# Full 128x128 weights for the routing's counts and broadcasts on TensorE, and two shifted fill lengths

## The chip, the cores and the metric

The kernel runs on one core of a Trainium2 chip. The metric is the device time of one execution in microseconds (us); lower is better. The kernel before takes 982.31 us (median of three runs, 982.09 to 982.40). The core has five engines that run beside each other and meet at semaphores: PE (TensorE, matrix products; its weight loads are listed apart as PEld), DVE (VectorE), ACT (ScalarE), POOL (GpSimd) and SP, which only issues transfers.

## The reference

Three stages follow each other: a linear attention, a gated FFN, and a mixture of experts with a greedy assignment. The change touches the routing of the third, cut here to what matters:

```python
def _moe2_ref(x, w_gate, w1, w2):            # x 2304x512, E = 8 experts
    cap = N // E                              # 288 tokens for each expert
    logits = x @ w_gate
    order = np.argsort(-logits.flatten())
    for idx in order:                         # best (token, expert) pair first
        tok, e = int(idx) // E, int(idx) % E
        if assigned[tok] >= 0 or counts[e] >= cap:
            continue
        assigned[tok] = e
        counts[e] += 1
    for e in range(E):
        mask = assigned == e
        out[mask] = np.maximum(x[mask] @ w1[e], 0.0) @ w2[e]
```

## The kernel before

The tokens lie in 18 chunks of 128 (NC = 18), a token to a partition. The greedy loop is replaced by seven phases (function `route`). Each phase finds, for every expert, the threshold of the logit from which its tokens fit into what is left of its capacity. The threshold's bits are found digit by digit, in six steps: two digits of 6 bits, then four of 5 bits. A step does this:

- DVE makes the candidate thresholds (`cand`) and compares every token's logit with all C of them (`ge`, 18 chunks of C columns; C is 62, 63 and then four times 31).
- PE counts: 18 matmuls (line 173), one for each chunk, with C columns of `ge` as weights and the chunk's 8 columns of `O` (which expert the token wants) as moving operand. They add up in `cnt`, C x 8.
- DVE compares the counts with the room left (`ok`, line 175).
- PE adds up the `ok` flags and spreads the sum to all 128 partitions in one matmul (line 179, `num`), with weights of C rows and 128 columns, all equal to the digit's unit (`pw`), or ones.
- DVE takes the maximum (`dig`): that is the digit, and the next step's candidates start from it.

After the six steps a phase ends with full 128x128 weights (`ones`, `li`): lines 201, 204 and 206, 19 matmuls that count tokens and settle ties.

While DVE works on a step, PE has something else to do. The last matmul of the FFN (line 903, 648 matmuls `py` with 128x512 moving operands) is a generator, `filler`. `route` yields a length in ns at each point where PE would wait, and `fill` puts so many matmuls of line 903 there, one for each 233 ns, carrying the rest over to the next yield. FILL holds the lengths: [0] ahead of a phase's first count, [1] ahead of the second count (63 columns), [2] ahead of the four counts of 31 columns, [3] between a count and its `num`, [4] ahead of line 201. PE, DVE and ACT run this part in the order in which it is written. Where the routing ends, what is left of the 648 matmuls runs, and then the experts start. POOL and SP are ordered by a scheduler.

`room` is a buffer of the pool that holds `xh` (the FFN's input); the routing keeps the 5-bit `ge` and its last one-hot matrices there. `us` and `li` are triangles, loaded with one DMA (`tri`) into a staging buffer `ws` and cast by POOL.

Of the kernel before, what the change touches and what calls it, by code (L numbers as in the profile page):

```python
# [9 lines left out]
F32 = mybir.dt.float32  # L10
F32R = mybir.dt.float32r
BF = mybir.dt.bfloat16
I32 = mybir.dt.int32
AF = mybir.ActivationFunctionType
OP = mybir.AluOpType
# [5 lines left out]
NT, DM, FF, E, FE = B * S, 512, 1536, 8, 1024  # L21
CAP = NT // E
NC = NT // 128
SL = 96
NJ = CAP // SL
NSL = NT // SL
BLK = 512
# [3 lines left out]
KD = DM // 128  # L31
# [4 lines left out]
W_SCALE = 2.0 ** -112  # L36
DIGITS = (6, 6, 5, 5, 5, 5)
SHIFTS = (26, 20, 15, 10, 5, 0)
FILL = (4900, 2450, 1800, 466, 1400, 3900, 5600)
FILL_MM = 233  # L40

DW = 3
# [58 lines left out]
def route(nc, keep, sb, ps, cst, L, R, ids, slot, aside, room):  # L101
# [7 lines left out]
    ones, us, li, cf, ci = cst["ones"], cst["us"], cst["li"], cst["cf"], cst["ci"]  # L109
    A3 = [128, NC, E]  # L110
    parts, off = [], 0
    for n in (31, NSL, SL, 2 * NSL):
        parts.append(room[:, off:off + NC * n].rearrange("p (c n) -> p c n", c=NC))
        off += NC * n
    ge5, oa, ob, rt = parts
    rt = rt.rearrange("p c (a n) -> p c a n", a=2)
    asg = keep.tile(A3, BF, name="asg")
    rem = keep.tile([128, E], F32, name="rem")
# [21 lines left out]
    def settle():  # L140
        pass

    s, O = best(True)
    for phase in range(E - 1):
        fb = None
        off = 0
        for step, (dg, sh) in enumerate(zip(DIGITS, SHIFTS)):
            C = (1 << dg) - (1 if step else 2)
            row = ci[:, off:off + C]
            off += C  # L150
            if step:
                cand = sb.tile([128, C], I32, name=f"cand{dg}")
                if step == 1:
                    nc.vector.tensor_tensor(cand, row, fb.to_broadcast([128, C]), op=OP.bitwise_xor)
                else:
                    nc.vector.tensor_scalar(cand, row, dig[:, :1], fb[:, :1], op0=OP.bitwise_xor,
                                            op1=OP.bitwise_xor)
                    nf = sb.tile([128, 1], I32, name="fb")
                row = cand
            ge = ge5 if dg == 5 else sb.tile([128, NC, C], BF, name=f"ge{dg}", bufs=1)  # L160
            cnt = ps.tile([64, 512], F32, name="cnt", bufs=1)
            nc.vector.tensor_tensor(ge, s.unsqueeze(2).to_broadcast([128, NC, C]),
                                    row.bitcast(F32).unsqueeze(1).to_broadcast([128, NC, C]), op=OP.is_ge)
            if step > 1:
                nc.vector.tensor_tensor(nf, fb, dig, op=OP.bitwise_xor)
                fb = nf
            if step:
                aside()
            else:
                settle()  # L170
            yield FILL[0] if step == 0 else FILL[1] if dg == 6 else FILL[2]
            for c in range(NC):
                nc.tensor.matmul(cnt[:C, :E], ge[:, c, :], O[:, c, :], start=(c == 0), stop=(c == NC - 1))  # L173
            ok = sb.tile([64, E], BF, name="ok")
            nc.vector.tensor_tensor(ok[:C], cnt[:C, :E], rem[:C], op=OP.is_ge)
            yield FILL[3]
            num = ps.tile([128, 512], F32, name="num", bufs=1)
            dig = sb.tile([128, 1], I32, name="dig")
            nc.tensor.matmul(num[:, :E], (cst["pow"][sh] if step else ones)[:C], ok[:C], start=True, stop=True)
            if step == 0:  # L180
                mx = sb.tile([128, 1], F32, name="mx")
                nc.vector.tensor_reduce(out=mx, in_=num[:, :E], axis=AX.X, op=OP.max)
                nc.vector.tensor_scalar(dig, mx, 1.0 - float(1 << (dg - 1)), float(1 << sh), op0=OP.add,
                                        op1=OP.mult)
                sg = sb.tile([128, 1], I32, name="sg")
                nc.vector.tensor_scalar(sg, dig, 31, 0x7FFFFFFF, op0=OP.arith_shift_right, op1=OP.bitwise_and)
                fb = sb.tile([128, 1], I32, name="fb")
                nc.vector.tensor_tensor(fb, dig, sg, op=OP.bitwise_xor)
            else:
                nc.vector.tensor_reduce(out=dig, in_=num[:, :E], axis=AX.X, op=OP.max)  # L190
        ti = sb.tile([128, 1], I32, name="ti")
        nc.vector.tensor_tensor(ti, fb, dig, op=OP.bitwise_xor)
        th = ti.bitcast(F32)
        A = sb.tile(A3, BF, name="A")
        Q = sb.tile(A3, BF, name="Q")
        nc.vector.scalar_tensor_tensor(A, bc(s), th, O, op0=OP.is_ge, op1=OP.mult)
        nc.vector.scalar_tensor_tensor(Q, bc(s), th, O, op0=OP.is_equal, op1=OP.mult)
        yield FILL[4]
        tot = ps.tile([128, 512], F32, name="cnt", bufs=1)
        totv = tot[:, :NC * E].rearrange("p (c e) -> p c e", e=E)  # L200
        nc.tensor.matmul(totv, ones, A, start=True, stop=True)
        suf = ps.tile([128, 512], F32, name="num", bufs=1)
        sufv = suf[:, :NC * E].rearrange("p (c e) -> p c e", e=E)
        nc.tensor.matmul(sufv, li, Q, start=True, stop=False)
        for c in range(1, NC):
            nc.tensor.matmul(sufv[:, :c, :], ones, Q[:, c:c + 1, :].to_broadcast([128, c, E]), start=False,
                             stop=(c == NC - 1))
        n = sb.tile([128, E], F32, name="n")
        ex = sb.tile([128, E], F32, name="ex")
        cl = sb.tile([128, E], F32, name="cl")  # L210
        ce = sb.tile([128, E], F32, name="ce")
        rj = sb.tile(A3, BF, name="rj")
        tk = sb.tile([128, NC], F32, name="tk")
        nc.vector.tensor_reduce(out=n, in_=totv.rearrange("p c e -> p e c"), axis=AX.X, op=OP.add)
        nc.vector.tensor_sub(ex, n, rem)
        nc.vector.tensor_scalar(cl, ex, 0.0, 100.0, op0=OP.is_ge, op1=OP.mult)
        nc.vector.tensor_scalar(ce, ex, 0.0, -BIG, op0=OP.is_ge, op1=OP.mult)
        nc.vector.tensor_tensor(R, R, be(cl), op=OP.max)
        nc.vector.tensor_tensor(L, L, be(ce), op=OP.add)
        nc.vector.tensor_tensor(rj, sufv, be(ex), op=OP.is_le)  # L220
        nc.vector.tensor_mul(rj, rj, Q)
        nc.vector.tensor_sub(A, A, rj)
        s, O = best(phase < E - 2)
        nc.vector.tensor_reduce(out=tk, in_=A, axis=AX.X, op=OP.max)
        nc.vector.scalar_tensor_tensor(gone, tk, -BIG, gone, op0=OP.mult, op1=OP.add)
        if phase < E - 2:
            nc.vector.tensor_add(s, s, gone)

        def settle(A=A, n=n, cl=cl):
            nc.vector.tensor_tensor(n, n, rem, op=OP.min)  # L230
            nc.vector.tensor_sub(rem, rem, n)
            nc.vector.scalar_tensor_tensor(rem, cl, 1e7, rem, op0=OP.mult, op1=OP.add)
            nc.vector.tensor_add(asg, asg, A)
# [3 lines left out]
    nc.vector.tensor_add(asg, asg, A)  # L237
    yield FILL[5]
    pre = ps.tile([128, 512], F32, name="num", bufs=1)
    prev = pre[:, :NC * E].rearrange("p (c e) -> p c e", e=E)  # L240
    nc.tensor.matmul(prev, us, asg, start=True, stop=False)
    for c in range(NC - 1):
        nc.tensor.matmul(prev[:, c + 1:, :], ones, asg[:, c:c + 1, :].to_broadcast([128, NC - 1 - c, E]),
                         start=False, stop=(c == NC - 2))
# [9 lines left out]
    for j in range(2, NJ):  # L254
# [7 lines left out]
                            op=OP.mult)  # L262
# [5 lines left out]
    for c in range(NC):  # L268
        nc.tensor.matmul(pi[:SL, :2 * NSL], ob[:, c, :], rt[:, c].rearrange("p a b -> p (a b)"), start=(c == 0),
                         stop=(c == NC - 1))  # L270
# [16 lines left out]
def kernel(ctx, tc, qT, kT, v1, om, wgv, rms, wo, wg2, w1, w2, cfd, trd, cid, out, dbg=None):  # L287
    nc = tc.nc
# [3 lines left out]
    stage = ctx.enter_context(tc.tile_pool(name="stage", bufs=3))  # L292
# [400 lines left out]
    ws = stage.tile([128, 2 * M], F32, name="ws")  # L693
# [93 lines left out]
    rp = fc.enter_context(tc.tile_pool(name="rp", bufs=2))  # L787
    psB = fc.enter_context(tc.tile_pool(name="psB", bufs=2, space=PSUM))
    ci = rp.tile([128, cid.shape[1]], I32, name="ci", bufs=1)
    ones, us, li = (rp.tile([128, 128], BF, name=n, bufs=1) for n in ("ones", "us", "li"))  # L790
    pw = {sh: rp.tile([128, 128], BF, name=f"pw{sh}", bufs=1) for sh in SHIFTS[1:]}
    nc.sync.dma_start(ci, cid)
    nc.gpsimd.memset(ones, 1.0)
    tri = stage.tile([128, 256], F32, name="ws")
    nc.sync.dma_start(tri, trd[:, :256])
    nc.gpsimd.tensor_copy(us, tri[:, :128])
    nc.gpsimd.tensor_copy(li, tri[:, 128:])
    for sh in pw:
        nc.gpsimd.memset(pw[sh], float(1 << sh))
    wos, hts = [], {}  # L800

    def wo_split(c):
# [17 lines left out]
    lates, step = [], 0  # L820
# [15 lines left out]
    while True:  # L836
# [5 lines left out]
        j, f, v = ffn_step_el()  # L842
# [94 lines left out]
        nc.sync.dma_start(dbg["L"].rearrange("(c p) e -> p c e", p=128), L)  # L937
    xg = {}
    room = xp.tile([128, KD * BLK], F32, name="xh").bitcast(BF)
    hot = xp.tile([128, TAIL, CAP], F32R, name="xl")  # L940

    def gather(e, j):
# [36 lines left out]
    sb = ctx.enter_context(tc.tile_pool(name="sb", bufs=2))  # L979
    ps = ctx.enter_context(tc.tile_pool(name="psC", bufs=2, space=PSUM))  # L980
# [141 lines left out]
```

## Time and profile before

| | |
|---|---|
| median of 3 runs | 982.31 us (982.09 to 982.40) |
| the profiled execution's own time | 982.99 us |
| its span, first to last instruction | 981.2 us |
| PE busy | 960.6 us, 98% of the span |
| DVE / ACT / POOL busy | 54% / 39% / 23% |
| routing (start of the first count to start of the last matmul of line 206) | 548.0 to 724.0 us |

The span is what the rows count in, from the first instruction. Between it and the execution's own time lie 1.8 us. A busy PE is not a PE at its peak: a matmul's length in the profile overlaps the next one's, so distances between starts tell more than lengths.

### The profile page before, as it was taken

The numbers are of one execution on the slowest core, as the hardware profiler recorded it, in microseconds if no ns is written. First come the engines' busy times: TensorE is split into PE (matmuls) and PEld (weight loads), VectorE is DVE, ScalarE is ACT, GpSimd is POOL, SyncE is SP. The second block draws the span as 40 slices with busy tenths as digits, with TensorE's granted clock in tenths as the row PEclk, the third lists the DMA queues.
The fourth block names the chain that finished last, engine by engine and source line by source line (L and its number), as shares of the span: only waits on it lengthen the run. The fifth ranks groups of instructions, "written<-read, shape, count | busy, mean of one in ns | idle before, by whom it ended". The sixth has DMA issues, their size and how long they took to land.

```text
span 981.2 us, 16610 instructions
## 1 busy us (share of the span) xinstructions
PE 960.6 (98%) x6419; PEld 812.5 (83%) x6419; DVE 526.5 (54%) x1199; ACT 384.4 (39%) x897; POOL 228.4 (23%) x278
## 2 busy tenths in 40 slices
PE   9998999999999999999999999999999999999996
PEld 7777789888788687777779777777778999999996
DVE  4899866556423463232244556566563555666652
ACT  6976646545433444122233110000003444444441
POOL 2375512112322225224333000000004211112111
PEclk9999999989999999999999999999999999999999
DMA  8457634543131217225665566666543566666550
GB/s 295 154 167 233 198 119 137 183 127 97 47 110 61 87 51 262 107 96 182 209 200 173 148 187 171 201 177 174 171 128 94 164 188 194 187 199 193 173 171 29
DMA packets 117151, 153.15 MB, mean 156 GB/s; under 512 B 8272, under 2 KB 78544, under 8 KB 117072
## 3 DMA queue, kind: packets, MB, share of 16 engines
q1 hardware_dynamic: 111264, 137.80, 45.3%
q0 software_dynamic: 3072, 9.44, 3.1%
q10 hardware_dynamic: 2736, 4.85, 1.3%
q8 instruction: 50, 0.82, 0.3%
q14 instruction: 29, 0.24, 0.1%
HBM read 108.03 MB, written 44.04 MB: 155 GB/s over the span
## 4 chain that ended last, share of the span: by engine, by line
PE 71%; issue 18%; DVE 5%; POOL 4%; ACT 1%; DMA 0%; POOLq 0%; SPq 0%; ACTq 0%; DVEq 0%
PE py L903 16%; PE gv L598 10%; PE gv L600 10%; PE gv L599 10%; PE pm L464 3%; PE pm L419 3%; PE cnt L173 2%; POOL out_dram L1031 2%; PE pm L460 2%; PE pp L373 1%; PE pp L378 1%; PE pp L375 1%; PE pp L374 1%; POOL xh L947 1%; DVE dw L531 1%
## 5 line engine op out<-in xcount | busy, mean ns | idle before, releaser
L598 PE MATMUL gv<-xh,wc 128*128 128x512 f32 (+1 forms) x480 | 185.9, 387 | 3.2 <-DVE th L610 2.4
L599 PE MATMUL gv<-xl,wc 128*128 128x512 f32 (+1 forms) x480 | 184.5, 384 | 0.9 <-DVE xl L506 0.9
L600 PE MATMUL gv<-xh,wc 128*128 128x512 f32 (+1 forms) x480 | 184.6, 385 | 0.0
L903 PE MATMUL py<-wc,ht 128*128 128x512 f32 x648 | 174.6, 407 | 0.0
L903 PEld LDWEIGHTS py<-wc,ht 128*128 128x128 f32 x648 | 114.2, 188 | 20.9
L598 PEld LDWEIGHTS gv<-xh,wc 128*128 128x128 f32 x480 | 91.4, 190 | 21.6 <-DVE th L610 2.6
L385 ACT ACTIVATE ft<-pp,mx 128x128 f32<-128x128 f32 (+1 forms) x320 | 92.5, 373 | 37.2 <-DVE mx L382 36.5
L599 PEld LDWEIGHTS gv<-xl,wc 128*128 128x128 f32 x480 | 91.2, 190 | 16.0 <-DVE xl L506 1.2
L600 PEld LDWEIGHTS gv<-xh,wc 128*128 128x128 f32 x480 | 91.2, 190 | 15.7
L610 DVE SCALAR_TENSOR_TENSOR th<-th,gv 128x512 f32<-128x512 f32 (+1 forms) x60 | 37.9, 632 | 97.1 <-ACT th L609 97.1
L625 POOL TENSOR_TENSOR hp<-th,hp 128x512 fp32r<-128x512 f32 (+1 forms) x48 | 57.4, 1196 | 136.3 <-ACT hp L624 121.8
L874 DVE TENSOR_TENSOR wc<-ws,wc 128x512 fp32r<-128x512 f32 x128 | 84.8, 683 | 0.0
L1009 PE MATMUL ph<-exh,wc 128*128 128x288 f32 x256 | 77.5, 303 | 0.8 <-issue 0.8
L1019 PE MATMUL py<-ehh,wc 128*128 128x288 f32 x256 | 77.7, 304 | 0.0
L1011 PE MATMUL ph<-exh,wc 128*128 128x288 f32 x256 | 76.1, 297 | 0.0
L1020 PE MATMUL py<-ehl,wc 128*128 128x288 f32 x256 | 75.9, 297 | 0.0
L1021 PE MATMUL py<-ehh,wc 128*128 128x288 f32 x256 | 75.9, 296 | 0.0
L1010 PE MATMUL ph<-exl,wc 128*128 128x288 f32 x256 | 75.8, 296 | 0.0
L914 ACT COPY ys<-py 128x512 f32<-128x512 f32 x18 | 10.6, 587 | 165.2 <-PE py L903 164.7
L382 DVE TENSOR_REDUCE mx<-pp 128x4 f32<-128x512 f32 (+2 forms) x88 | 56.0, 637 | 29.9 <-PE pp L375 22.5
L884 ACT CAST wc<-ws 128x1024 fp32r<-128x1024 f32 x64 | 66.9, 1046 | 2.4 <-ACT ys L914 2.4
L622 DVE SCALAR_TENSOR_TENSOR th<-gv,th 128x512 f32<-128x512 f32 (+1 forms) x48 | 30.0, 624 | 53.2 <-PE gv L600 52.9
(199 smaller groups left out, 1802.5 us busy)
## 6 DMA issues: line engine op xcount, KB each, us to landing
ws<-in_w_dram SPq DMA_DIRECT2D x64, 512.0 KB, 3.6
ht<-h_dr SPq DMA_DIRECT2D x54, 512.0 KB, 4.1
h_dr<-hp SPq DMA_DIRECT2D x36, 512.0 KB, 2.8
ws<-in_wgv_dram SPq DMA_DIRECT2D x24, 512.0 KB, 4.5
h_dr<-hp SPq DMA_DIRECT2D x24, 256.0 KB, 2.9
ws<-in_wo_dram SPq DMA_DIRECT2D x12, 512.0 KB, 3.8
h_dr<-ht SPq DMA_DIRECT2D x12, 512.0 KB, 3.0
y_dr<-ys ACTq DMA_DIRECT2D x18, 256.0 KB, 4.3
```

What stands on the lines that cost most here:

```text
L385: nc.scalar.activation(ft[:n, g], pp[:n, g], AF.Exp, bias=mx[:n, g:g + 1])
L598: nc.tensor.matmul(pg[:, :n], w[:, 0, v, k], xh[:, k, :n], start=(k == 0), stop=False)
L599: nc.tensor.matmul(pg[:, :n], w[:, 0, v, k], xl[:, k, :n], start=False, stop=False)
L600: nc.tensor.matmul(pg[:, :n], w[:, 1, v, k], xh[:, k, :n], start=False, stop=(k == KD - 1))
L874: nc.vector.tensor_sub(w[:, 1, h], sv[:, h], w[:, 0, h])
L903: nc.tensor.matmul(py, ht[:, i4, a], w[:, l, f % 2], start=(f == 0 and n == 0), stop=(f == KF - 1 and n == 2))
L1009: nc.tensor.matmul(ph, w[:, 0, k, m], xh[:, k], start=(k == 0), stop=False)
L1010: nc.tensor.matmul(ph, w[:, 0, k, m], xl[:, k], start=False, stop=False)
L1011: nc.tensor.matmul(ph, w[:, 1, k, m], xh[:, k], start=False, stop=(k == KD - 1))
L1019: nc.tensor.matmul(py, w[:, 0, k], hh[:, k], start=(k == 0), stop=False)
L1020: nc.tensor.matmul(py, w[:, 0, k], hl[:, k], start=False, stop=False)
L1021: nc.tensor.matmul(py, w[:, 1, k], hh[:, k], start=False, stop=(k == KE - 1))
```

## The change

The counts use 128 columns as weights whatever C is: chunk c's slice starts at column c x C as before and runs on into the columns of the chunks behind it (the last ones into a zeroed pad). The rows of `cnt` from C on hold sums that belong to no candidate. The `num` weights have 128 rows, with zeros from row C on, so that those rows count for nothing. For this `ge` of the 6-bit steps is one lasting buffer, `pw` gets a sixth member, POOL clears the pads, and `us` and `li` move into `room`, with their load and casts written later in the program. FILL[1] goes from 2450 to 2700 and FILL[2] from 1800 to 1740.

```diff
-FILL = (4900, 2450, 1800, 466, 1400, 3900, 5600)
+FILL = (4900, 2700, 1740, 466, 1400, 3900, 5600)
...
-    for n in (31, NSL, SL, 2 * NSL):
+    for n in (NSL, SL, 2 * NSL):
...
-    ge5, oa, ob, rt = parts
+    oa, ob, rt = parts
+    ges = {5: room[:, off:off + (NC - 1) * 31 + 128],
+           6: sb.tile([128, (NC - 1) * 63 + 128], BF, name="ge6", bufs=1)}
+    for g in ges.values():
+        nc.gpsimd.memset(g, 0.0)
...
-            ge = ge5 if dg == 5 else sb.tile([128, NC, C], BF, name=f"ge{dg}", bufs=1)
-            cnt = ps.tile([64, 512], F32, name="cnt", bufs=1)
+            gw = ges[dg]
+            ge = gw[:, :NC * C].rearrange("p (c n) -> p c n", c=NC)
+            cnt = ps.tile([128, 512], F32, name="cnt", bufs=1)
...
-                nc.tensor.matmul(cnt[:C, :E], ge[:, c, :], O[:, c, :], start=(c == 0), stop=(c == NC - 1))
-            ok = sb.tile([64, E], BF, name="ok")
-            nc.vector.tensor_tensor(ok[:C], cnt[:C, :E], rem[:C], op=OP.is_ge)
+                nc.tensor.matmul(cnt[:, :E], gw[:, c * C:c * C + 128], O[:, c, :], start=(c == 0), stop=(c == NC - 1))
+            ok = sb.tile([128, E], BF, name="ok")
+            nc.vector.tensor_tensor(ok, cnt[:, :E], rem, op=OP.is_ge)
...
-            nc.tensor.matmul(num[:, :E], (cst["pow"][sh] if step else ones)[:C], ok[:C], start=True, stop=True)
+            nc.tensor.matmul(num[:, :E], cst["pow"][sh], ok, start=True, stop=True)
...
-    for sh in pw:
-        nc.gpsimd.memset(pw[sh], float(1 << sh))
+    for n, (dg, sh) in enumerate(zip(DIGITS, SHIFTS)):
+        nc.gpsimd.memset(pw[sh], 0.0)
+        nc.gpsimd.memset(pw[sh][:(1 << dg) - (1 if n else 2)], float(1 << sh) if n else 1.0)
...
+    us, li = (room[:, i:i + 128] for i in (2 * KD * BLK - 256, 2 * KD * BLK - 128))
+    tri = stage.tile([128, 256], F32, name="ws")
+    nc.sync.dma_start(tri, trd[:, :256])
+    nc.gpsimd.tensor_copy(us, tri[:, :128])
+    nc.gpsimd.tensor_copy(li, tri[:, 128:])
```

On PE the first phase shows the change best: from the first `num` to the first count of 31 columns. The rows are PE's program; `ge_...` and `xh` are the comparison matrices, `pw_...` the weights of `num`, and where "..." stands the pair of load and matmul repeats. Before:

```order
L903 MATMUL py<-wc,ht 128x512 x2
L179 LDWEIGHTS ones
L179 MATMUL num<-ok,ones 128x8
L903 MATMUL py<-wc,ht 128x512 x10
L173 LDWEIGHTS ge_5583
L173 MATMUL cnt<-oh,ge_5583 63x8
...
L903 MATMUL py<-wc,ht 128x512 x2
L179 LDWEIGHTS pw_4435
L179 MATMUL num<-ok,pw_4435 128x8
L903 MATMUL py<-wc,ht 128x512 x8
L173 LDWEIGHTS xh
L173 MATMUL cnt<-oh,xh 31x8
```

And the same place of the change, whose lines 178, 184 and 905 are 173, 179 and 903 of before:

```order
L905 MATMUL py<-wc,ht 128x512 x2
L184 LDWEIGHTS pw_4433
L184 MATMUL num<-ok,pw_4433 128x8
L905 MATMUL py<-wc,ht 128x512 x11
L178 LDWEIGHTS ge_5513
L178 MATMUL cnt<-oh,ge_5513 128x8
...
L905 MATMUL py<-wc,ht 128x512 x2
L184 LDWEIGHTS pw_4434
L184 MATMUL num<-ok,pw_4434 128x8
L905 MATMUL py<-wc,ht 128x512 x8
L178 LDWEIGHTS xh
L178 MATMUL cnt<-oh,xh 128x8
```

The number of instructions is the same, the counts write 128 rows instead of 63 or 31, and eleven filler matmuls stand ahead of the second count where ten stood (twelve for eleven in every other phase). Ahead of the counts of 31 columns 7 or 8 stand as before, with more sevens. All 648 of line 903 remain.

On POOL, in the FFN's last block, ahead of the routing, the split of `hp` (the hidden layer's low part) runs for each half of the FFN's width. Before, ten of them stand in a row:

```order
L625 TENSOR_TENSOR hp<-th,hp 128x256 x10
```

With the change the casts of the triangles stand behind the third of them:

```order
L630 TENSOR_TENSOR hp<-th,hp 128x256 x3
L945 CAST xh<-ws 128x128
L946 CAST xh<-ws 128x128
L630 TENSOR_TENSOR hp<-th,hp 128x256 x7
```

So the two casts moved from the place where `ones` is set, some 130 us earlier, to a place where seven splits wait behind them.

## Rows read from the trace of the kernel before

**Rows 1.** The page's head: span, busy time of PE and PEld.

```profile
span 981.2 us, 16610 instructions
PE 960.6 (98%) x6419; PEld 812.5 (83%) x6419; DVE 526.5 (54%) x1199; ACT 384.4 (39%) x897; POOL 228.4 (23%) x278
```

**Rows 2.** Busy time of each engine in stretches (us), the stretch of the routing.

```profile
543.50:727.50 184.00, 184.00 (x1508) 133.17 (x1508) 108.04 (x383) 15.86 (x23) 0.92 (x2) 1.00 0.61 175
```

**Rows 3.** The counts, line 173: duration in ns min/median/max, first and last start.

```profile
L173 PE MATMUL cnt<-oh,xh x504: 166/166/181, 555.5 to 721.0; 128*31 128x8 bf16 x168
...
L173 PE MATMUL cnt<-oh,ge x252: 172/172/194, 548.0 to 707.7; 128*62 128x8 bf16 x63, 128*63 128x8 bf16 x63
```

**Rows 4.** Timeline of PE, one 5-bit step: start, us, instruction, number merged.

```profile
555.14 0.39 PE L903 MATMUL py<-wc,ht 128*128 128x512 f32 x1
555.46 0.61 PE L173 MATMUL cnt<-oh,xh 128*31 128x8 bf16 x18
555.99 0.73 PE L903 MATMUL py<-wc,ht 128*128 128x512 f32 x2
556.66 0.17 PE L179 MATMUL num<-ok,pw 31*128 31x8 bf16 x1
556.76 1.91 PE L903 MATMUL py<-wc,ht 128*128 128x512 f32 x7
558.60 0.26 PE L173 MATMUL cnt<-oh,xh 128*31 128x8 bf16 x4
```

**Rows 5.** Timeline of PE, the two 6-bit steps of the first phase.

```profile
548.02 0.72 PE L173 MATMUL cnt<-oh,ge 128*62 128x8 bf16 x18
...
549.33 0.18 PE L179 MATMUL num<-ok,ones 62*128 62x8 bf16 x1
549.44 2.55 PE L903 MATMUL py<-wc,ht 128*128 128x512 f32 x10
551.97 0.74 PE L173 MATMUL cnt<-oh,ge 128*63 128x8 bf16 x18
...
553.31 0.18 PE L179 MATMUL num<-ok,pw 63*128 63x8 bf16 x1
```

**Rows 6.** Timeline of PE, the phase's end, with weights of 128x128.

```profile
567.90 0.40 PE L903 MATMUL py<-wc,ht 128*128 128x512 f32 x1
568.14 0.24 PE L201 MATMUL cnt<-A,ones 128*128 128x144 bf16 x1
...
568.27 0.78 PE L206 MATMUL num<-Q,ones 128*128 128x8 bf16 x17
...
569.18 4.70 PE L903 MATMUL py<-wc,ht 128*128 128x512 f32 x20
573.80 0.26 PE L173 MATMUL cnt<-oh,ge 128*62 128x8 bf16 x3
```

**Rows 7.** Line 206: seven of its matmuls on the timeline, and all its durations.

```profile
568.30 0.34 PE L206 MATMUL num<-Q,ones 128*128 128x16 bf16 x7
...
L206 PE MATMUL num<-Q,ones x119: 169/194/223, 568.3 to 724.0; 128*128 128x8 bf16 x7, 128*128 128x16 bf16 x7, 128*128 128x24 bf16 x7, 128*128 128x32 bf16 x7
```

**Rows 8.** Timeline of DVE, what stands between a `num` and the next count.

```profile
550.58 1.34 DVE L162 TENSOR_TENSOR ge<-s,cand 128x1134 bf16<-128x1134 f32 x1
...
556.87 0.17 DVE L190 TENSOR_REDUCE dig<-num 128x1 int32<-128x8 f32 x1 [0.62 <-PE num L179]
...
557.41 0.74 DVE L162 TENSOR_TENSOR xh<-s,cand 128x558 bf16<-128x558 f32 x1
```

**Rows 9.** Timeline of PE, the only weights of 96 columns in bf16.

```profile
734.23 0.99 PE L269 MATMUL cnt<-xh 128*96 128x48 bf16 x18
```

**Rows 10.** Timelines of POOL and SP where memsets, casts and the triangles' load go.

```profile
394.09 1.29 POOL L625 TENSOR_TENSOR hp<-th,hp 128x512 fp32r<-128x512 f32 x1 [2.98 <-issue]
...
523.42 1.47 POOL L625 TENSOR_TENSOR hp<-th,hp 128x256 fp32r<-128x256 f32 x1 [1.62 <-ACT hp L624]
...
518.31 1.02 SPq L865 DMA_DIRECT2D ws<-in_w_dram  x1
```

**Rows 11.** Timelines of DVE and PE where the filler ends and the experts begin.

```profile
742.87 0.48 DVE L968 TENSOR_SCALAR xh<-xh,here 96x512 f32<-96x512 f32 x1 [0.27 <-DMA xh<-y_dr,idc]
...
744.01 0.41 PE L992 MATMUL gv<-cf,xh 96*128 96x96 f32 x3
```

More of the change, by code (lines that the diff above doesn't have):

```diff
@@ L789 @@
     ci = rp.tile([128, cid.shape[1]], I32, name="ci", bufs=1)
-    ones, us, li = (rp.tile([128, 128], BF, name=n, bufs=1) for n in ("ones", "us", "li"))
-    pw = {sh: rp.tile([128, 128], BF, name=f"pw{sh}", bufs=1) for sh in SHIFTS[1:]}
+    ones = rp.tile([128, 128], BF, name="ones", bufs=1)
+    pw = {sh: rp.tile([128, 128], BF, name=f"pw{sh}", bufs=1) for sh in SHIFTS}
     nc.sync.dma_start(ci, cid)
     nc.gpsimd.memset(ones, 1.0)
[L794 to L797, printed above, removed]
-    for sh in pw:
-        nc.gpsimd.memset(pw[sh], float(1 << sh))
+    for n, (dg, sh) in enumerate(zip(DIGITS, SHIFTS)):
+        nc.gpsimd.memset(pw[sh], 0.0)
+        nc.gpsimd.memset(pw[sh][:(1 << dg) - (1 if n else 2)], float(1 << sh) if n else 1.0)
     wos, hts = [], {}
```

## The prediction

> **What bounds the kernel now.** I read the page's head first: PE is busy for 960.6 of 981.2 us [rows 1]. Then the busy times by stretch: from 543.5 to 727.5, which holds the whole routing, PE is busy for 184.00 of 184.00 us at full granted clock, DVE for 108 [rows 2]. So PE sets the pace there, and the filler matmuls of line 903 do what they are for. But busy is not dense: what counts is the distance between starts. In undisturbed filler, 20 matmuls start from 569.18 on and the next instruction starts at 573.80 [rows 6]; taking off the last distance of 0.32 (below), 19 distances make 573.80 - 0.32 - 569.18 = 4.30 us, or 0.227 each. Every extra over 0.227 per filler is what the routing costs PE, and the filler's number is fixed, so each us of it that goes shortens the kernel.
>
> **What an insertion costs, narrow and full.** Line 173 has 756 matmuls, 42 bursts of 18: 28 with 31 columns, 7 each with 62 and 63 [rows 3]. Inside a burst of 31 columns they start every (0.61 - 0.17) / 17 = 0.026 us [rows 4]. The edges are dear: the burst starts 0.32 after the filler ahead of it (555.14 to 555.46) instead of 0.227, and the `num` behind it starts 0.67 after the first of two fillers (555.99 to 556.66) instead of 0.454 [rows 4].
>
> Lines 201 to 206 are the same kind of insertion with full 128x128 bf16 weights. They start 0.24 after the filler (567.90 to 568.14). The last of the 17 matmuls starts at 568.27 + 0.78 - 0.22 = 568.83, and the second filler behind it at 569.18, 0.35 later [rows 6, 7]. In the burst of 31 columns the same distance is 0.10 + 0.34 = 0.44: the last starts at 555.46 + 0.61 - 0.17 = 555.90, the second filler at 555.99 + 0.73 - 0.39 = 556.33 [rows 4]. So narrow weights in rows or columns cost about 0.08 at the way in and 0.09 at the way out, and full ones don't. [...]
>
> Does a wider weight cost more to load? Seven matmuls of line 206 with moving operands of 16 to 64 columns take 0.34 in all, the last about 0.19 of it: (0.34 - 0.19) / 6 = 0.025 a pair of load and matmul [rows 7]. That is no more than the 0.026 of 31 columns, and less than what 62 and 63 columns take, (0.72 - 0.17) / 17 = 0.032 and (0.74 - 0.17) / 17 = 0.034 [rows 5]. I take 0.025 for the new burst. [...]
>
> **The sum.** I count by the distances that the rows give.
> - Count to `num`: now 555.46 to 556.66 = 1.20 with 31 columns, 548.02 to 549.33 = 1.31 with 62, 551.97 to 553.31 = 1.34 with 63 [rows 4, 5]. New: 17 x 0.025 + 0.35 + 0.24 = 1.015. Gain: 28 x 0.185 + 7 x 0.295 + 7 x 0.325 = 9.5 us.
> - `num` to a count of 31 columns, 28 times: now 556.66 to 558.60 = 1.94 over 7 fillers [rows 4]. New with as many: 0.35 + 5 x 0.227 + 0.24 = 1.725. Gain 0.215, 6.0 us in all. (Of it 0.17 are the two edges; the rest is that fillers after a narrow insertion start a little over 0.227 apart.)
> - `num` to the count of 63 columns, 7 times: now 549.33 to 551.97 = 2.64 over 10 fillers; new over 10: 0.35 + 8 x 0.227 + 0.24 = 2.41. Gain 0.23, 1.6 us, if PE finds work for it; that is FILL[1], below.
> - `num` to line 201, 7 times: only the way out is narrow, 0.09, 0.6 us. The way into a phase's first count, 7 times 0.08: 0.6 us.
>
> Together 18.3 us. Rounding of rows to 0.01 and the entries, which I see between 0.23 and 0.24, make this 17.5 to 19.5.
>
> **What the fills do.** DVE needs a fixed time between a `num` and the next count. For 63 columns, `ge` ends at 550.58 + 1.34 = 551.92 [rows 8] and the burst starts at 551.97, 2.64 after its `num`: PE is already waiting for DVE there. With ten fillers the faster PE would wait 2.64 - 2.41; the new FILL[1] puts eleven or twelve there, which last 0.35 + 9 x 0.227 + 0.24 = 2.63 or 2.86. So at most 0.01 is waited, and the 1.6 us count. For 31 columns `ge` ends at 557.41 + 0.74 = 558.15 [rows 8], with 0.05 as above 1.54 after its `num` at 556.66. Seven fillers last 1.725: 0.185 to spare, where 0.40 were. FILL[2] makes some eights sevens; that moves fillers, not work. Between a count and its `num` the way shrinks from 556.66 - 555.90 = 0.76 to 0.35 + 0.24 = 0.59; DVE, which has to compare the counts in between, idles for 0.62 behind that compare now [rows 4, 8], so 0.45 are left.
>
> **What is hidden.** POOL gets seven more small memsets and a clear around 390, and is idle for 2.98 ahead of its next work at 394.09 [rows 10]; the second clear stands ahead of a split at the end of the FFN's fourth block. Were either late by 1 us, a split would be, once. The casts go behind the split that ends ahead of 523.42, where POOL is idle for 1.62 [rows 10]; they wait for the triangles' load, which SP issues in the place of the load at 518.31 [rows 10], three splits earlier. If that load were late, the casts would hold POOL and with it the seven splits behind, whose low parts PE multiplies; 1 us at most, once. DVE's compare on 128 partitions has the same 8 columns. At the far end the gathered rows are ready at 742.87 + 0.48 = 743.35 and PE comes at 744.01 [rows 11]; one filler fewer stands behind the routing, 0.23 of 0.66 to spare.
>
> The profiled execution took 982.99, 1.8 over its span and 0.7 over the median. 982.99 - 18.3 = 964.7, and on the median's scale **964.0 us**.
>
> **Rivals.**
> 1. *The loads of `ge` are slow (0.06).* All full bf16 weights of the trace start at a buffer's aligned start; a chunk of 31 or 63 columns begins at an odd column. If such loads aren't as quick as those of line 206, they follow the rows of narrower ones: 0.034 at 63 columns, (0.99 - 0.20) / 17 = 0.046 at 96 [rows 9], a straight line to 0.059 at 128. 42 bursts x 17 x 0.034 = 24 us more than forecast: 988 us, slower (0.04). If only the odd starts of 35 bursts suffer, 35 x 9 x 0.034 = 11 us: 975 us (0.02). It decides from 0.051 a pair on. Against it: loads of 31 columns already start at odd columns and lose nothing.
> 2. *PE waits for DVE in the 5-bit steps (0.10).* The spare time falls from 0.40 to 0.185. If the step's chain is 0.1 to 0.2 over that, by a longer DVE row or a dig that starts later after a full matmul, 28 waits give 3 to 5.5 back: 967 to 969.5 us.
> 3. *The edges stay (0.03).* If it is the change of type or operand that costs 0.08 and 0.09, and not the shape, only the pace inside the 6-bit bursts is gained: 7 x 17 x (0.007 + 0.009) = 1.9 us, 982.3 - 1.9 = 980.4, on the limit of no change. Against it: lines 201 to 206 are bf16 after f32 too.
>
> **How the numbers follow.** The forecast has 0.81: 964.0, with its own range 962.5 to 966. To hold 8 in 10 with the second rival's cases, which are the nearest, I reach from 962.0 to 969.0. Faster than before by over 0.2%, 2 us, which is about what a measurement of this kernel can tell: the forecast, the second rival and the half of the first, 0.93. Within 0.2%: 0.03. Slower: 0.04.
>
> **What would show it.** Right: bursts of line 178 starting 0.23 to 0.24 after a filler, their 18 matmuls 0.025 apart in every step, `num` about 1.0 after its count; PE still without idle time from 543 to 727 and everything from the experts on shifted by 18 us. Wrong: pairs over 0.03 apart with 128 columns (rival 1), PE's weight load idle on DVE's `ge` in the 5-bit steps (rival 2), or a burst that still starts 0.32 after its filler (rival 3).

## The result, and the profile after

The changed kernel takes 964.75 us (median of four runs, 964.56 to 968.68) beside 982.26 for the kernel before: ratio 0.983, 95% interval 0.981 to 0.986. It is 17.5 us faster, where 18.3 less than before, 964.0, had been forecast. By the interval alone the gain is 14 to 19 us; what tells 17 from 18 is the rows below. The profiled execution took 964.78.

The page's head, and the stretch of the routing among the busy times by stretch (its end moved from 727.5 to 710):

```profile
span 963.0 us, 16617 instructions
...
PE 943.2 (98%) x6419; PEld 805.2 (84%) x6419; DVE 526.8 (55%) x1199; ACT 384.6 (40%) x897; POOL 231.0 (24%) x287
...
543.50:710.00 166.50, 166.50 (x1509) 125.58 (x1509) 108.24 (x382) 15.87 (x23) 0.93 (x2) 1.00 0.67 193
```

PE is still busy all the time there, with as many instructions as in [rows 2] (1509 against 1508) in 17.5 us less. DVE has the same work in less time. The counts, listed by their line:

```profile
L178 PE MATMUL cnt<-oh,xh x504: 166/166/180, 554.8 to 704.0; 128*128 128x8 bf16 x168
...
L178 PE MATMUL cnt<-oh,ge x252: 166/166/180, 548.1 to 692.6; 128*128 128x8 bf16 x126
```

A single matmul with 128 columns lasts what one with 31 lasted, 166 ns, and less than the 172 of one with 62 or 63 [rows 3]. The gain is in the distances between their starts. PE's timeline, a 5-bit step, which answers to [rows 4]:

```profile
553.66 1.29 PE L905 MATMUL py<-wc,ht 128*128 128x512 f32 x5
554.79 0.61 PE L178 MATMUL cnt<-oh,xh 128*128 128x8 bf16 x18
555.26 0.71 PE L905 MATMUL py<-wc,ht 128*128 128x512 f32 x2
555.81 0.18 PE L184 MATMUL num<-ok,pw 128*128 128x8 bf16 x1
555.85 1.86 PE L905 MATMUL py<-wc,ht 128*128 128x512 f32 x7
557.55 0.61 PE L178 MATMUL cnt<-oh,xh 128*128 128x8 bf16 x18
```

Count to `num` is 1.02 (554.79 to 555.81) where it was 1.20, and `num` to the next count over seven fillers 1.74 (555.81 to 557.55) where it was 1.94. The burst begins 553.66 + 1.29 - 0.39 = 554.56 to 554.79 = 0.23 after the filler ahead of it, where it was 0.32. And the 6-bit steps of the first phase, which answer to [rows 5]:

```profile
548.14 0.61 PE L178 MATMUL cnt<-oh,ge 128*128 128x8 bf16 x18
...
549.16 0.18 PE L184 MATMUL num<-ok,pw 128*128 128x8 bf16 x1
549.20 2.75 PE L905 MATMUL py<-wc,ht 128*128 128x512 f32 x11
551.82 0.61 PE L178 MATMUL cnt<-oh,ge 128*128 128x8 bf16 x18
...
552.84 0.18 PE L184 MATMUL num<-ok,pw 128*128 128x8 bf16 x1
```

Both counts reach their `num` in 1.02, as with 31 columns; they took 1.31 and 1.34. Ahead of the second count stand eleven fillers, and 2.66 pass (549.16 to 551.82), a little over the 2.64 that DVE needs.

### The profile page after: what moved, and what is told of

Read it like the earlier page. It is cut to its first block, busy times and chain, and to the rows that moved or that the text cites. A ratio compares the mean times of both kernels' runs of the same rounds, so it can differ in the third digit from the quotient of the medians.

```text
span 963.0 us, 16617 instructions
## 1 busy us (share of the span) xinstructions
PE 943.2 (98%) x6419; PEld 805.2 (84%) x6419; DVE 526.8 (55%) x1199; ACT 384.6 (40%) x897; POOL 231.0 (24%) x287
## 4 chain that ended last, share of the span: by engine, by line
PE 71%; issue 18%; DVE 5%; POOL 4%; ACT 1%; DMA 0%; POOLq 0%; SPq 0%; ACTq 0%; DVEq 0%
PE py L905 16%; PE gv L603 10%; PE gv L605 10%; PE gv L604 10%; PE pm L469 3%; PE pm L424 3%; POOL out_dram L1038 2%; PE cnt L178 2%; PE pm L465 2%; PE pp L378 1%; PE pp L383 1%; PE pp L380 1%; PE pp L379 1%; POOL xh L954 1%; DVE dw L536 1%
## 5 line engine op out<-in xcount | busy, mean ns | idle before, releaser
L905 PE MATMUL py<-wc,ht 128*128 128x512 f32 x648 | 167.3, 404 | 0.0
```

What stands on the lines that cost most here:

```text
L905: nc.tensor.matmul(py, ht[:, i4, a], w[:, l, f % 2], start=(f == 0 and n == 0), stop=(f == KF - 1 and n == 2))
```

## Experiments

All stand against one measure beside the total: the time from the start of the first count to the start of the experts' first transpose, read off the timelines. On PE it holds the counts, the `num`, lines 201 to 206, the token lists and 621 of the 648 fillers, the same number in every run, and nothing else. Totals scatter more than the effects of most runs: the kernel before spread from 979.08 to 984.79 in 16 executions on the chip of runs 1 to 4, and from 983.21 to 988.61 in 13 on that of runs 5 to 8, which is some 3 us up. So the stretch decides. It is read from one profiled execution of each kernel; that of the change is 178.70, and 178.72 when it ran again on the second chip (run 9). The kernel before was profiled only once.

| run | first count to experts, us | total, us | before on that chip | ratio, 95% interval |
|---|---|---|---|---|
| before | 548.02 to 744.01: 195.99 | 982.26 | | |
| the change | 548.14 to 726.84: 178.70 | 964.75 | 982.26 | 0.983 (0.981 to 0.986) |
| 1 counts full, num narrow | 186.67 | 973.02 | 982.25 | 0.991 (0.988 to 0.994) |
| 2 num full, counts narrow | 187.93 | 975.56 | 982.25 | 0.994 (0.992 to 0.997) |
| 3 all narrow, rest of the change | 195.95 | 982.24 | 982.25 | 1.000 (0.998 to 1.002) |
| 4 fill lengths of before | 179.52 | 966.74 | 982.25 | 0.984 (0.982 to 0.987) |
| 5 counts 64 columns | 191.47 | 984.30 | 985.97 | 0.998 (0.997 to 1.000) |
| 6 counts 65 columns | 183.82 | 976.04 | 985.97 | 0.991 (0.989 to 0.993) |
| 7 counts 127 columns | 202.67 | 994.45 | 985.97 | 1.010 (1.008 to 1.011) |
| 8 num 65 rows | 178.78 | 969.25 | 985.97 | 0.984 (0.982 to 0.985) |
| 9 the change again | 178.72 | 968.48 | 985.19 | 0.983 (0.980 to 0.985) |
| 10 line 274 full too | 178.13 | 967.43 | 985.19 | 0.981 (0.979 to 0.983) |

Each edit is shown against the changed kernel.

**1. Counts full, num narrow.**

```diff
-nc.tensor.matmul(num[:, :E], cst["pow"][sh], ok, start=True, stop=True)
+nc.tensor.matmul(num[:, :E], cst["pow"][sh][:C], ok[:C], start=True, stop=True)
```

Expected: 

> Counts with 128 columns, num as before with 31, 62 or 63 rows; everything else as in the change. My theory (each insertion pays at its two edges for its own narrowness): the 42 count bursts give 28 x 0.18 + 7 x 0.29 + 7 x 0.31 = 9.3 us and the num keep their edges, so 982.3 - 9.3 = 973.0 us, 972 to 974; counts start 0.23 after a filler, num still 0.33. Rival (what counts is going from narrow weights to full ones anywhere in a step, so one narrow insertion spoils the step): little is gained, 978 us or more.

PE's timeline:

```profile
558.33 0.61 PE L178 MATMUL cnt<-oh,xh 128*128 128x8 bf16 x18
558.80 0.71 PE L905 MATMUL py<-wc,ht 128*128 128x512 f32 x2
559.44 0.17 PE L184 MATMUL num<-ok,pw 31*128 31x8 bf16 x1
```

The total is 973.02, as forecast, and the stretch 9.32 shorter. The `num` begins 559.44 - (558.80 + 0.71 - 0.39) = 0.32 after the second filler, as before: its edge is its own.

**2. Num full, counts narrow.** The counts take C columns and write C rows, and `ok` is one lasting buffer cleared once, so that its other rows are zero.

```diff
+    ok = keep.tile([128, E], BF, name="ok")
+    nc.vector.memset(ok, 0.0)
...
-nc.tensor.matmul(cnt[:, :E], gw[:, c * C:c * C + 128], O[:, c, :], start=(c == 0), stop=(c == NC - 1))
+nc.tensor.matmul(cnt[:C, :E], gw[:, c * C:c * C + C], O[:, c, :], start=(c == 0), stop=(c == NC - 1))
```

Expected: 

> The num with 128 rows, counts as before with 31, 62 or 63 columns (the flags' other rows are zero); everything else as in the change. My theory: the 42 num give 42 x 0.19 = 8.0 us, plus up to 1 us from fillers that run closer together behind them: 973.3 to 974.5 us. Together with the run with full counts the gains add up to the change's 17.5. Rival (the counts are all that matters): 980 us or more.

The stretch is 8.06 shorter, the 8.0 of the 42 `num`; the up to 1 us more behind them did not come. The total, 975.56 (975.26 to 977.82), lies 1.1 over the expected range; in the profiled execution 0.56 more than in the change's lies ahead of the first count and 0.61 behind the stretch. Runs 5 to 7, which have the lasting `ok` too, also lose 0.6 to 0.7 over the experts; the cause is open. On the timeline the `num` begins 0.24 after its filler (559.41 + 0.73 - 0.39 = 559.75 to 559.98):

```profile
559.41 0.73 PE L906 MATMUL py<-wc,ht 128*128 128x512 f32 x2
559.98 0.18 PE L185 MATMUL num<-ok,pw 128*128 128x8 bf16 x1
```

The two halves add up: 9.32 + 8.06 = 17.38, and the whole change shortens the stretch by 17.29.

**3. All weights narrow, everything else as in the change** (the edits of 1 and of the counts in 2 together, with `ok` written in C rows).

Expected: 

> All weights as narrow as before, but the pads, the memsets, the moved triangles and both new fill lengths of the change. My theory: none of these moves the end, because PE never waits in the routing either way: 982.3 us, within 0.5. In the steps ahead of 63 columns the 0.05 wait of some phases goes (at most 0.2 us in all). Rival (the fill lengths are a part of the gain): 980.5 or less, or, if the shorter fill makes PE wait, 983 or more.

195.95 against 195.99, and the same total (982.24 against 982.25, known to 0.2%, 2 us). So the pads and the fill lengths are worth nothing by themselves inside the routing. The memsets and the moved casts run ahead of the first count, where the stretch cannot price them. The first count starts at 548.02 in the profile of before and from 548.14 to 549.16 in those of the change and runs 1 to 4, which all have these memsets and casts; so a cost of some tenths of a us is not ruled out. For the splits of `hp` on POOL the changed kernel's timeline shows what the casts cost:

```profile
522.80 0.29 POOL L945 CAST xh<-ws 128x128 bf16<-128x128 f32 x1 [0.83 <-DMA ws<-in_tri_dram]
523.04 0.29 POOL L946 CAST xh<-ws 128x128 bf16<-128x128 f32 x1
523.59 1.47 POOL L630 TENSOR_TENSOR hp<-th,hp 128x256 fp32r<-128x256 f32 x1 [0.26 <-ACT hp L629]
```

The cast waits 0.83 for the triangles' transfer, and the split behind it still has 0.26 of idle time ahead of it, which ACT ends. It starts 0.17 later than before (523.42 in [rows 10]), and an earlier split, ahead of both the clear of `room` and the casts, is already 0.20 later (493.75 to 493.95). The split behind that clear starts 0.27 later (500.09 to 500.36), so the clear costs it under 0.1.

**4. The change with the fill lengths of before.**

```diff
-FILL = (4900, 2700, 1740, 466, 1400, 3900, 5600)
+FILL = (4900, 2450, 1800, 466, 1400, 3900, 5600)
```

Expected: 

> The change with FILL[1] and FILL[2] of before (2450 and 1800). My theory: in the phases with ten fillers ahead of the 63-column count PE now waits for DVE, 2.64 - 2.41 = 0.23 each in four of seven phases, 0.9 us; elsewhere nothing: 965.6 us, 965.2 to 966.0, and PE's weight load idle on DVE's comparison there. Rival (the fill lengths don't matter): 964.7 us.

The stretch is 0.82 longer than the change's. PE's weight loads, a phase with ten fillers:

```profile
550.18 2.16 PEld L905 LDWEIGHTS py<-wc,ht 128*128 128x128 f32 x10
552.84 0.52 PEld L178 LDWEIGHTS <-ge 128*128 128x128 bf16 x18 [0.50 <-DVE ge L167]
```

and the same place in the changed kernel, with eleven:

```profile
551.81 0.52 PEld L178 LDWEIGHTS <-ge 128*128 128x128 bf16 x18 [0.29 <-DVE ge L167]
```

0.50 against 0.29: 0.21 of waiting for DVE's comparison, in four phases of seven. FILL[2] has no part in the 0.82: from a `num` to a count of 31 columns seven fillers take 1.74 and eight 1.97 in both runs (medians). The total, 966.74 (965.37 to 968.38), is too scattered to show 0.8 by itself.

**5. Counts of 64 columns** (62, 63 and 31 widened to 64; with the cleared `ok` of 2).

```diff
-nc.tensor.matmul(cnt[:, :E], gw[:, c * C:c * C + 128], O[:, c, :], start=(c == 0), stop=(c == NC - 1))
+nc.tensor.matmul(cnt[:64, :E], gw[:, c * C:c * C + 64], O[:, c, :], start=(c == 0), stop=(c == NC - 1))
```

Expected: 

> The change, but the counts take 64 columns in every step instead of 128 (num stay full; the flags' other rows are zero). [...] Rival (the pad alone brings the gain): 965 us.

**6. Counts of 65 columns**, the same edit with 65.

Expected: 

> The same with 65 columns, one more than 64. [...]

**7. Counts of 127 columns**, the same edit with 127.

Expected: 

> The same with 127 columns. My theory: the quick load needs all 128; edges cheap, the pair follows the straight line from 63 and 96 columns to 0.058: 42 x 17 x 0.0325 = 23 us over the change, 988 us, 985 to 990, slower than before. [...] Rival (127 columns load as quickly as 128): 965 us.

PE's timelines. With 64 columns:

```profile
560.17 1.86 PE L906 MATMUL py<-wc,ht 128*128 128x512 f32 x7
561.96 0.74 PE L180 MATMUL cnt<-oh,xh 128*64 128x8 bf16 x18
562.63 0.73 PE L906 MATMUL py<-wc,ht 128*128 128x512 f32 x2
```

With 65:

```profile
555.71 0.39 PE L906 MATMUL py<-wc,ht 128*128 128x512 f32 x1
555.94 0.73 PE L180 MATMUL cnt<-oh,xh 128*65 128x8 bf16 x18
556.52 0.71 PE L906 MATMUL py<-wc,ht 128*128 128x512 f32 x2
```

With 127:

```profile
558.59 1.86 PE L906 MATMUL py<-wc,ht 128*128 128x512 f32 x7
560.29 1.17 PE L180 MATMUL cnt<-oh,xh 128*127 128x8 bf16 x18
561.31 0.71 PE L906 MATMUL py<-wc,ht 128*128 128x512 f32 x2
```

The edges turn between 64 and 65 columns. With 64 the burst begins 561.96 - (560.17 + 1.86 - 0.39) = 0.32 after its filler, with 65 and 127 it begins 0.23 after (555.71 to 555.94; 560.29 - 560.06). From the last matmul of the burst to the second filler behind it 0.44 pass with 64 (562.53 to 562.97), 0.34 with 65 (556.50 to 556.84) and with 127 (561.29 to 561.63). The pace follows the width: (0.74 - 0.17) / 17 = 0.033 at 64 and 65, (1.17 - 0.17) / 17 = 0.059 at 127, on the straight line from 63 and 96 columns (0.034 and 0.046). At 128 it is (0.61 - 0.17) / 17 = 0.026. So one column more than 127 cuts the distance to less than half, and one more than 64 removes the edges; the two turn at different widths. Against the change the stretches are 12.77, 5.12 and 23.97 longer, where 13, 6 and 23 were expected. These are estimates from the edges and paces in [rows 4 to 6, 9]: 42 x (0.09 + 0.09 + 17 x 0.0075) with 64 columns, for the edges of a narrow burst and 0.033 a pair; 42 x 17 x 0.0085 with 65, for 0.034 a pair without the edges; 42 x 17 x 0.0325 with 127, for 0.058. That the edges end between 64 and 65 no row of before shows; runs 5 and 6 do. Run 7 is slower than the kernel before, by 1.0%. The rivals (the pad alone brings the gain; whatever is short of 128 pays the edges; 127 are as quick as 128) fall.

The totals of these three runs, and of runs 8 and 9, lie 3.8 to 6.8 us over what was expected (977.5, 970.8 and 988 for runs 5 to 7, 964.7 for runs 8 and 9), above the range wherever one was given (976 to 979, 970 to 972, 985 to 990, and 0.4 about 964.7 in run 8). The kernel before is 2.9 to 3.7 up on that chip. In the profiles the excess lies outside the stretch: 0 to 3.5 us more than in the change's profile ahead of the first count, and 1.8 to 4.8 more behind the stretch (last section). In run 5 the total is only 1.7 below the kernel before, with a stretch 4.5 shorter; as the kernel before has no profile on that chip, this stays unexplained.

**8. Num of 65 rows.**

```diff
-nc.tensor.matmul(num[:, :E], cst["pow"][sh], ok, start=True, stop=True)
+nc.tensor.matmul(num[:, :E], cst["pow"][sh][:65], ok[:65], start=True, stop=True)
```

Expected: 

> The change, but num takes 65 of its 128 rows (the rows from there on are zero in the weights anyway). [...] Rival (every weight short of 128 rows pays): 42 x 0.19 = 8 us over the change, 972.7 us.

```profile
558.75 0.71 PE L905 MATMUL py<-wc,ht 128*128 128x512 f32 x2
559.30 0.18 PE L184 MATMUL num<-ok,pw 65*128 65x8 bf16 x1
```

The `num` begins 0.23 after its filler (559.07 to 559.30), and the stretch is the change's within 0.08, as was expected. The limit in rows lies between 63, where the `num` of the kernel before starts 0.33 after its filler (578.76 to 579.09), and 65; 64 rows were not tried. The total is 4.5 over the change's; in the profiled execution 0.73 more lies ahead of the first count and 3.99 behind the stretch, and 0.08 in it.

**9 and 10. The change again, and line 274 full too.** Line 274 makes the token lists with weights of 96 columns; here they run on into the next chunk, and one filler more covers a wait for DVE.

```diff
-FILL = (4900, 2700, 1740, 466, 1400, 3900, 5600)
+FILL = (4900, 2700, 1740, 466, 1400, 3900, 5833)
...
-nc.tensor.matmul(pi[:SL, :2 * NSL], ob[:, c, :], rt[:, c].rearrange("p a b -> p (a b)"), start=(c == 0),
+nc.tensor.matmul(pi[:, :2 * NSL], room[:, NC * NSL + c * SL:NC * NSL + c * SL + 128], rt[:, c].rearrange("p a b -> p (a b)"), start=(c == 0),
```

Expected of 9: 

> The changed kernel once more, beside the next one on one chip. 964.7 us on a chip on which the kernel before takes 982.3; from the last transpose of the ranks to the experts' first transpose 183.3 us, as before.

Expected of 10: 

> The change, and with it line 274 (18 matmuls that make the token lists, weights of 96 columns, 0.046 apart) on 128 columns that run on into the next chunk, and FILL[6] 5833 instead of 5600, one filler more where PE waits 0.2 for DVE. My theory: the pair falls to 0.026, 17 x 0.020 = 0.35 us, and the wait of 0.2 goes: 0.5 us less than the change, to be seen in the stretch from the ranks to the experts (182.7 to 182.9 instead of 183.3), hardly in the totals. Rival (with a moving operand of 48 columns the load isn't what sets the pace): the pair stays at 0.046 and only the 0.2 goes.

Run 10, PE's timeline, to be held against [rows 9]:

```profile
722.97 0.62 PE L274 MATMUL cnt<-xh 128*128 128x48 bf16 x18
723.44 0.47 PE L905 MATMUL py<-wc,ht 128*128 128x512 f32 x1
```

The 18 matmuls and the way to the next filler take 0.47 (722.97 to 723.44) instead of 0.83 (734.23 to 735.06 before): they start 0.026 apart instead of 0.046, and the rival falls. From the last transpose of the ranks to the experts it is 182.73 (549.21 to 731.94) where run 9 has 183.32 (543.53 to 726.85), both as expected. From the first count the stretch is 178.13 against 178.72 of run 9 on the same chip: 0.59, expected 0.5. It is the fastest version of the routing here; in totals that spread over 5 us and more, 0.6 can't be seen (967.43 against 968.48).

## Why the prediction was right

**What bounds it: right.** PE is busy for all of the stretch before and after, and what is taken from an insertion goes off the end.

**The edges and the pace: right, each by itself.** Counts alone gain 9.32, `num` alone 8.06 (runs 1 and 2). What makes the edge of these bf16 weights is their shape: it stands with 31 and 64 columns and is gone with 65 (0.32 in [rows 4] and run 5, 0.23 in run 6), and it stands with 63 rows and is gone with 65 (0.33 before, 0.23 in run 8). What fills the 0.09 no run shows. The prediction had only full against narrow for it. The pace was taken as 0.025 and is 0.026.

The limit is not one of shape alone. The trace of before has f32 weights of only 16 columns among the same fillers:

```profile
540.66 1.09 PE L903 MATMUL py<-wc,ht 128*128 128x512 f32 x4
541.59 0.28 PE L636 MATMUL lg<-hp,wog 128*16 128x256 f32 x1
541.71 0.39 PE L903 MATMUL py<-wc,ht 128*128 128x512 f32 x1
```

They start 0.23 after their filler (540.66 + 1.09 - 0.39 = 541.36 to 541.59), and the next filler 0.12 after them, with a moving operand half as long as a filler's: no edge on either side. So narrow and bf16 together pay here, narrow f32 and full bf16 do not; why the type matters was not tested.

**The sum: 18.3 in the routing was 1.0 too much.** It measured 17.29, just under the 17.5 to 19.5 given for it. The way from a count to its `num` is not where it failed: its median over the 42 steps is 1.01 (1.015 was taken), and it gave 9.7 of the forecast 9.5 us. The term that was mis-sized is the way from a `num` to the next count. With 0.227 taken for each filler, it gave 5.4 of 6.0 us ahead of the counts of 31 columns and 1.2 of 1.6 ahead of those of 63. The prediction priced all 28 steps of the first kind by a row with seven fillers. In the kernel before 21 of them had eight; here is one, and one of the changed kernel:

```profile
559.80 0.17 PE L179 MATMUL num<-ok,pw 31*128 31x8 bf16 x1
559.91 2.12 PE L903 MATMUL py<-wc,ht 128*128 128x512 f32 x8
561.96 0.21 PE L173 MATMUL cnt<-oh,xh 128*31 128x8 bf16 x2
...
558.56 0.18 PE L184 MATMUL num<-ok,pw 128*128 128x8 bf16 x1
558.60 2.09 PE L905 MATMUL py<-wc,ht 128*128 128x512 f32 x8
560.53 0.61 PE L178 MATMUL cnt<-oh,xh 128*128 128x8 bf16 x18
```

Over eight fillers the medians are 2.15 before and 1.97 now, a gain of 0.18, and over seven 1.94 and 1.74, a gain of 0.20, where 0.215 was counted each time. Likewise the three phases that had eleven fillers ahead of the count of 63 columns took 2.81 before, 0.17 and not a whole filler more than the 2.64 of ten, and their twelve take 2.91 now (2.86 was forecast). The way into a phase's first count gave 0.4 of 0.6.

That the profiled spans differ by 18.2, as forecast, is partly chance: the span of before holds a wait of some 1.0 us in the first expert that the span of after lacks (last section). The closeness of the total, 964.75 to 964.0, has luck in it too, since single executions scatter by more than that.

**The fill lengths: right.** They give back 0.82 that PE would wait for DVE (run 4; forecast 0.9), and nothing by themselves (run 3).

**What is hidden: right.** The casts wait 0.83 for their load, and no split is seen to be late for it (run 3).

**Rival 1 (slow loads) fell**, but its price was real: a load one column short of full costs what it says (run 7, 24 us for the 24 forecast). Odd starts cost nothing: counts of 31 and 63 columns start at odd columns in every other chunk and run at 0.026. **Rival 2 (PE waits for DVE in the 5-bit steps)** didn't happen: counts start 0.23 after their filler there, and the weight loads that DVE's comparison releases idle 0.27 on average, as those that wait for nothing do (0.26). **Rival 3 (the edges stay)** fell with the change's own rows, 0.23 where 0.32 stood, and with runs 5 and 6, where one column more removes the edges while type and operands stay.

## What to carry to other kernels

Where a few small matmuls stand between large ones, read the distance from the last large matmul to the first small one and back: bf16 weights of 31 to 64 columns, or 31 to 63 rows, cost about 0.09 us at each edge here, among f32 fillers, and their narrowness saves nothing (31 columns start 0.026 apart, and so do 128). Widen them to the full 128x128 with zeros or with neighbours whose results are dropped, and do it fully: 65 columns only remove the edges (0.23, but 0.033 a pair), and 127 start more than twice as far apart as 128 (0.059 against 0.026). When PE gets faster, lengthen the cover where it already waits for DVE (0.82 us in run 4).

## What was not expected

A wait of PE in the first expert, some 12 us after its first transposes, differs from execution to execution and stands ahead of the same matmul each time. In the profile of before:

```profile
756.23 0.29 PE L1011 MATMUL ph<-exh,wc 128*128 128x288 f32 x1
757.32 0.40 PE L1009 MATMUL ph<-exh,wc 128*128 128x288 f32 x1 [0.80 <-issue]
```

That is 1.09 from start to start, where 0.13 is usual. The profiles of the change and of runs 1 to 4 have no such gap. All six of the second chip have one, of 1.76 us (run 9) to 2.61 (run 7) from start to start. That of run 8 shows 2.24 us of idle time, and behind it a stretch at a granted clock of 0.50 (the third column from the end) where PE is busy throughout:

```profile
741.49 0.71 ACT L1019 ACTIVATE ehh<-ph 128x288 fp32r<-128x288 f32 x2 [3.91 <-PE ph L1018]
742.45 0.40 PE L1016 MATMUL ph<-exh,wc 128*128 128x288 f32 x1 [2.24 <-DVE ehl L1020]
...
743.50:746.50 3.00, 3.00 (x14) 3.00 (x14) 0.46 (x1) 1.34 (x2) 0.00 (x0) 0.50 0.00 0
750.00:753.00 3.00, 3.00 (x27) 3.00 (x26) 1.75 (x3) 1.14 (x3) 0.00 (x0) 1.00 0.40 96
```

PE makes 14 matmuls in the first 3 us, where the later ones have 27 at a granted clock of 1.00. Such a stretch at 0.50 follows the pause in the profiles of runs 5, 7, 8 and 10, and not in those of runs 6 and 9. Pause and slow stretch together put run 8 4.0 us behind the change's profile there, and the pause alone run 9 1.75; this is much of why the profiled executions of the second chip are longer, and why the stretch was used. What comes late first in run 8's trace is ACT's activation of `ph`: it starts at 741.49, 4.32 after the one before, where 1.60 is the distance in the change's profile. What delays it stays open: no run was made for it.
